# First two weight sets of a fused attention and two-layer gated MLP kernel, issued from ScalarE's DMA queue

## The chip, the cores and the metric

The kernel runs on one core of one Trainium2 chip. The metric is the device time of one execution in microseconds. Three timed runs of the kernel before gave 963.62 to 964.25 us, median 963.83 us.

## The reference, cut to what matters

Three stages, all in float32. Inputs `q`, `k`, `v` are (4, 8, 576, 64), and the five weight matrices are stored as 64-bit floats.

```python
# stage 1: attention, twice, then added
q_d, k_d, v_d = mean over groups of 4 positions            # 144 positions
out_d     = softmax(q_d @ k_d.T / 8) @ v_d                 # pooled attention
out_local = softmax(where(|i - j| < 4, q @ k.T / 8, -1e9)) @ v
x = repeat(out_d, 4) + out_local                           # -> (2304, 512)
# stage 2: gated layer, d_ff = 1536
g = x @ w_gate
y = (silu(g) * (x @ w_val)) @ w_out                        # (2304, 512)
# stage 3: leaky layer, d_ff = 2048
h = y @ w_in
out = (max(h, 0) + alpha * min(h, 0)) @ w2_out
```

## The kernel before, in words

Attention is cut into 32 units; unit `n` is half of the positions (288) of a pair of heads of one batch. Four units make one block of 288 tokens by 512 features, the input `xh`, `xl` of the gated layer (each float32 value is held as a high and a low float32r part, so that every product is three matmuls, `mm3`). The gated layer runs block by block, and within a block over 12 weight sets `j`. A set is three 512 KB loads: `g` (128 columns of `w_gate`), `v` (of `w_val`), `o` (128 rows of `w_out`). Before TensorE can use a loaded piece, `w_split` turns its 64-bit floats into the two parts: two passes on ScalarE (lines 129 and 137), one on VectorE (139), a copy on ScalarE (142) and a subtraction on GpSimd or VectorE (143). The split weights stay in SBUF for all eight blocks, so loading and splitting happen once, in the first 130 us or so; sets 0 to 3 have SBUF of their own, the later ones lie where data of the first eight units lay (`pslot`), and can be loaded only as these units finish.

The first eight units run before or beside block 0. Units 0 to 3 go through three loops in turn: transposes and scores (`a_T`, `a_QK`, `a_QE`), softmax (`a_EXP`, `a_NRM`), and the products with `v` (`a_vd`, `a_PT`, `a_PV`). Units 4 to 7 then run one after the other (`a_all`). Each unit needs its keys and queries (`a_load`), its pooled values (`a_load_v`), and windows of `v` (`a_load_w`, in the trace `qv<-vwin`), which are read from a DRAM buffer `vwin` that `stage` fills first by DRAM-to-DRAM copies. At the end `a_PV` writes `xh` and `xl`.

Order. All loads are issued by SyncE (`nc.sync`, in the trace `SPq`) on one queue, except two small copies at the start that ScalarE issues. The string `lo` in line 20 gives the order in which the first loads are written: `a` keys and queries of units 0 to 3, `s` and `t` the two halves of batch 0's `vwin`, `v` pooled values, `w` windows of units 0 to 3, `b` queries of units 4 to 7, `0` and `1` the weight sets 0 and 1, `x` windows of units 4 to 7, `2` and `3` the sets 2 and 3. The engines' instruction streams are in order; the stream of each engine is laid out by a list scheduler, which takes instructions by their place in the program as they become ready by its own estimates. `issue_after(i)` keeps what is inside it behind instruction `i` on the engine that issues `i`. `gate(n, stage)` notes the last VectorE, GpSimd and ScalarE instruction of unit `n` at the end of its scores (stage 0) or its softmax (stage 1); the splits of sets 0 and 1 stand behind the gates of unit 3, stage 1, on all three engines (`gD`, `gP`, `gA` are 8 for them). Sets 4 to 9, the load of `alpha`, batch 1's `vwin` and the loads of unit 8 (`load8`) follow on the same queue; sets 10 and 11, and the `vwin` copies of batches 2 and 3, are written after the tenth set has been split.

PSUM is shared: the banks of unit 3 (`gv`) become the banks of the first `g` and `v` products of the gated layer, so block 0 cannot begin before unit 3's product has been read.

Of the kernel before, what the change touches and what calls it, by code (L numbers as in the profile page):

```python
# [16 lines left out]
DRAM = bass.MemoryType.DRAM  # L17


K = dict(kdP=0, qdP=0, dnP=2, ldn=9, lo='asvtwb01x23', NPRO=8, c=5, a1=1, a2=0, OFF=25, oT=3, oE=3, oP=5, oV=12, vd1=2, vd2=1, pre=(0, 2, 0, 0), lo1=0, lo2=1, nst=3, nrm=0, sub=0, nrm1=0, sub1=0, qtA=0, ldw=1, xl1=0, ly=4, l2=3, st2=2, early=1, w2p=1, la=0, bdV=0, sp=9, s2=0, s3=0, gj=7, gs=1, vr=0, kc=0, gD=(8, 8, 0, 0, 0, 0), gP=(8, 8, 8, 8, 0, 0), gA=(8, 8, 0, 0, 0, 0))  # L20


@with_exitstack
def attn_moe_moe2_kernel(
# [13 lines left out]
    nc = tc.nc  # L38
# [24 lines left out]
    wp = ctx.enter_context(tc.tile_pool(name="wp", bufs=1))  # L63
# [33 lines left out]
    wdma = {}  # L97
    W = {}

    def w_load(kind, j, slot, pool=wp):  # L100
        t = raw[slot] = pool.tile([128, 512, 2], I32, tag=slot, name="raw", bufs=1)
        src = wsrc[kind]
        if kind in ("o", "o2"):
            r = nc.sync.dma_start(out=t.rearrange("p f t -> p (f t)"), in_=src[j * 128:(j + 1) * 128, :])
        else:
            r = nc.sync.dma_start(
                out=t.rearrange("p f t -> p (f t)").rearrange("p (k f) -> p k f", k=KD),
                in_=src[:, j * 256:(j + 1) * 256].rearrange("(k p) f -> p k f", p=128))
        wdma[slot] = r.ins
# [44 lines left out]
    def coords(n):  # L154
        blk, hp = divmod(n, NP)
        b, half = divmod(blk, 2)
        return b, half, hp, blk

    order = [f"{kind}{j}" for j in range(F1 - 8, F1) for kind in "gvo"]
    st_slots = order[5 * NP:][:K["nst"]]  # L160
    NEARLY = F1 - 2
    pslot = {(what, n): order[4 * i + n] for i, what in enumerate(("qv", "qs", "kn", "vd", "bd")) for n in range(NP)}
    for n in range(NP):
        pslot["qv", n + NP] = pslot["kn", n]
        pslot["qs", n + NP] = pslot["qs" if K["vr"] else "vd", n]
    NPRO = K["NPRO"]
    srs = [ap_.tile([128, 8], F32, name=f"sr{i}", bufs=1) for i in range(4)]
# [120 lines left out]
    def a_T(n, A):  # L288
# [24 lines left out]
        else:  # L313
            for r in range(NW):
                nc.tensor.transpose(A[:, 0, QB * r:QB * (r + 1)], d["qn"][:, r].rearrange("p h c -> p (h c)"), idn)
            if K["qtA"]:
                nc.scalar.copy(out=qT[:, 0:HB], in_=A[:, 0, 0:HB])
# [18 lines left out]
    def a_vd(n):  # L336
        b, half, hp, blk = coords(n)
        if n < NPRO and K["vr"]:
            return
        if half == 0:  # L340
            vs = vss[hp] = ap_.tile([72, 2, 2, D], F32, tag=f"vs{hp}", name="vs", bufs=1)
            for f in range(2):
                if n < NP:
                    nc.vector.reduce_sum(vs[:, f], hu[n]["vd"][f].rearrange("p h (r c) -> p h c r", r=4), axis=AX.X)
                    continue
                vv = hu[n]["vd"][f].rearrange("p h (r c) -> p h r c", r=4)
                nc.gpsimd.tensor_tensor(out=vv[:, :, 0:2], in0=vv[:, :, 0:2], in1=vv[:, :, 2:4], op=ALU.add)
                nc.gpsimd.tensor_tensor(out=vs[:, f], in0=vv[:, :, 0], in1=vv[:, :, 1], op=ALU.add)
# [10 lines left out]
    def a_QK(n, A):  # L359
        b, half, hp, blk = coords(n)  # L360
        d = hu[n]
        qT, kT, qd, kd = d["qT"], kTs[hp], d["qd"], kds[hp]
        with behind(n):
            for w in range(NW):
                for h in range(2):
                    hs = slice(64 * h, 64 * h + 64)
                    for i in range(NS):
                        q0 = QB * w + SUB * i
                        k0 = half * HB + q0
                        nc.tensor.matmul(A[SWIN * i:SWIN * (i + 1), h, w * SWIN:(w + 1) * SWIN],  # L370
                                         qT[hs, q0:q0 + SWIN], kT[hs, k0:k0 + SWIN], start=True, stop=True)
            for h in range(2):
                hs = slice(64 * h, 64 * h + 64)
                nc.tensor.matmul(A[:72, h, LW:SW], qd[hs], kd[hs], start=True, stop=True)

    def a_QE(n, A):
        half, d = coords(n)[1], hu[n]
        sm = late(n, "sm", [128, 2, SW])
        mx = d["mx"] = ap_.tile([128, 8], F32, tag="mx", name="mx", bufs=4)
        d["A"] = A  # L380
        mk = mask[:, half:half + 3].rearrange("p w j -> p (w j)").unsqueeze(1).to_broadcast([128, 2, LW])
        nc.vector.tensor_tensor(out=sm[:, :, 0:LW], in0=A[:, :, 0:LW], in1=mk, op=ALU.add)
        nc.vector.reduce_max(mx[:72, 6:8], A[:72, :, LW:SW], axis=AX.X)
        loc = d["loc"] = sm[:, :, 0:LW].rearrange("p h (w j) -> p h w j", w=NW)
        m4 = mx[:, 0:6].rearrange("p (h w) -> p h w", h=2)
        nc.vector.tensor_reduce(out=m4, in_=loc, axis=AX.X, op=ALU.max)
        d["act"] = K["a1" if n < 2 * NP else "a2"]
        d["la"] = n < NPRO and K["la"]
        if d["la"]:
            lb = d["lb"] = ap_.tile([128, 8], F32, tag="lb", name="lb", bufs=4)  # L390
            nc.vector.tensor_scalar(out=lb[:, 0:6], in0=mx[:, 0:6], scalar1=-scale, scalar2=None, op0=ALU.mult)
        if d["act"]:
            nb = d["nb"] = ap_.tile([72, 4], F32, tag="nb", name="nb", bufs=4)
            nc.vector.tensor_scalar(out=nb, in0=mx[:72, 4:8], scalar1=-scale / 16.0, scalar2=None, op0=ALU.mult)
        else:
            nc.vector.tensor_tensor(out=sm[:72, :, LW:SW], in0=A[:72, :, LW:SW],
                                    in1=mx[:72, 6:8].unsqueeze(2).to_broadcast([72, 2, SD]), op=ALU.subtract)
        if not d["la"]:
            (nc.vector if K["sub1" if n < NPRO else "sub"] else nc.gpsimd).tensor_tensor(out=loc, in0=loc, in1=m4.unsqueeze(3).to_broadcast([128, 2, NW, SWIN]), op=ALU.subtract)

    def a_EXP(n):
        d = hu[n]
        sm, A = d["sm"], d["A"]
        sr = d["sr"] = srs[n % 4]
        if d["act"]:
            for h in range(2):
                nc.scalar.activation(out=sm[:72, h, LW:SW], in_=A[:72, h, LW:SW], func=AF.Exp, scale=scale / 16.0,
                                     bias=d["nb"][:, 2 + h:3 + h], accum_out=sr[:72, 6 + h:7 + h])
        if d["la"]:
            for h in range(2):  # L410
                for w in range(NW):
                    c = NW * h + w
                    nc.scalar.activation(out=d["loc"][:, h, w], in_=d["loc"][:, h, w], func=AF.Exp, scale=scale,
                                         bias=d["lb"][:, c:c + 1], accum_out=sr[:, c:c + 1])
        else:
            nc.scalar.activation(out=sm[:, :, 0:LW], in_=sm[:, :, 0:LW], func=AF.Exp, scale=scale)
        if not d["act"]:
            nc.scalar.activation(out=sm[:72, :, LW:SW], in_=sm[:72, :, LW:SW], func=AF.Exp, scale=scale / 16.0)
# [92 lines left out]
            if kk == 1 and live:  # L511
                tick(6, HB)

    def load1(j):
        for kind in "gvo":
            w_load(kind, j, f"{kind}{j}")

    gates = {}

    def gate(n, stage):  # L520

        bb = tc.nc.cur_bb.bb.instructions
        for key, eng in (("D", nc.vector), ("P", nc.gpsimd), ("A", nc.scalar)):
            gates[key, n, stage] = next(i for i in reversed(bb) if i.engine == eng.engine)
# [613 lines left out]
    gs = {}  # L1138
# [171 lines left out]
    if True:  # L1310
# [65 lines left out]
        for n in range(NP):  # L1376
            a_T(n, P[n])
            a_QK(n, P[n])
            a_QE(n, P[n])
            gate(n, 0)  # L1380
        for n in range(NP):
            a_EXP(n)
            a_NRM(n)
            gate(n, 1)
        for n in range(NP):
            with tc.issue_after(gates["D", NP - 1, 0]):
                a_vd(n)
            a_PT(n, P[n])
            a_PV(n, P[n])
# [18 lines left out]
        for j in range(4, F1 - 2):  # L1408
            load1(j)
# [30 lines left out]
        OFF = K["OFF"]  # L1440
        at(0 if NPRO == NP else OFF - 7, lambda: a_pre(NPRO))
        for n in range(NPRO, NHU):
            if n < 2 * NP:
                c = K["c"]
                p, oT, oE, oP, oV = c * (n - NP) + 1, 1, 1, c - 1, c
            else:
                p, oT, oE, oP, oV = OFF + K["sp"] * (n - 2 * NP), K["oT"], K["oE"], K["oP"], K["oV"]
# [150 lines left out]
```

## Time and profile before

| what | value |
|---|---|
| median of 3 runs | 963.83 us |
| profiled execution | 963.16 us, its span 961.4 us |
| TensorE matmul busy | 923.8 us (96%) |
| VectorE, ScalarE, GpSimd busy | 627.4, 430.6, 370.9 us |
| granted TensorE clock, mean | 0.988 |
| DMA | 116.25 MB, mean 121 GB/s |

The profiled execution is 0.67 us under the median. TensorE works nearly all the time over the whole span; in the first eighth it does not, and the other engines and the DMA are at their busiest there. Views by stretch and the chain of waits tell more than the shares of the whole span, because the change touches loads of the first part alone.

### The profile page before, as it was taken

The numbers are of one execution on the slowest core, as the hardware profiler recorded it, in microseconds if no ns is written. First come the engines' busy times: TensorE is split into PE (matmuls) and PEld (weight loads), VectorE is DVE, ScalarE is ACT, GpSimd is POOL, SyncE is SP. The second block draws the span as 40 slices with busy tenths as digits, with TensorE's granted clock in tenths as the row PEclk, the third lists the DMA queues.
The fourth block names the chain that finished last, engine by engine and source line by source line (L and its number), as shares of the span: only waits on it lengthen the run. The fifth ranks groups of instructions, "written<-read, shape, count | busy, mean of one in ns | idle before, by whom it ended". The sixth has DMA issues, their size and how long they took to land.

```text
span 961.4 us, 20968 instructions
## 1 busy us (share of the span) xinstructions
PE 923.8 (96%) x8258; PEld 869.4 (90%) x8258; DVE 627.4 (65%) x1215; ACT 430.6 (45%) x965; POOL 370.9 (39%) x492
## 2 busy tenths in 40 slices
PE   6689889999999999999999998999999999999998
PEld 4478789999999999999999998999999988888887
DVE  5887775556454555545443365777767899688885
ACT  4698732222232222322222356664345775545553
POOL 7488863233422244322222278856161930000000
PEclk9689999999999999999999999999999999999999
DMA  7999741123111141111101346234426873445331
GB/s 193 267 339 364 178 104 28 37 66 63 43 46 24 35 92 36 35 41 22 49 10 39 111 137 210 109 119 156 161 111 213 294 280 97 154 142 164 113 110 44
DMA packets 162089, 116.25 MB, mean 121 GB/s; under 512 B 98889, under 2 KB 143177, under 8 KB 161225
## 3 DMA queue, kind: packets, MB, share of 16 engines
q1 hardware_dynamic: 161927, 114.92, 39.7%
q8 instruction: 64, 1.05, 0.5%
q14 instruction: 34, 0.28, 0.1%
q10 hardware_dynamic: 64, 0.01, 0.0%
HBM read 86.58 MB, written 34.60 MB: 126 GB/s over the span
## 4 chain that ended last, share of the span: by engine, by line
PE 82%; DMA 5%; SPq 4%; POOL 3%; DVE 2%; ACT 2%; issue 2%; DVEq 0%; POOLq 0%; ACTq 0%
PE y L1214 5%; PE y L503 5%; PE y L505 4%; PE g L505 4%; PE v L503 4%; PE y L504 4%; PE g L503 4%; PE g L504 4%; PE v L505 4%; PE c L1214 4%; PE v L504 4%; PE y L1013 3%; PE y L1014 3%; PE y L1015 3%; PE c L1013 3%; PE c L1014 3%
## 5 line engine op out<-in xcount | busy, mean ns | idle before, releaser
L547 DVE SCALAR_TENSOR_TENSOR u<-u,g 128x288 f32<-128x288 f32 x90 | 40.7, 452 | 134.0 <-ACT u L546 133.9
L503 PE MATMUL g<-xh,w 128*128 128x288 f32 x360 | 108.7, 302 | 10.9 <-DVE u L547 5.5
L505 PE MATMUL g<-xh,w 128*128 128x288 f32 x360 | 107.9, 300 | 1.2 <-POOL w L143 1.2
L504 PE MATMUL g<-xl,w 128*128 128x288 f32 x360 | 107.8, 299 | 0.0
L503 PE MATMUL v<-xh,w 128*128 128x288 f32 x360 | 107.6, 299 | 0.1
L504 PE MATMUL v<-xl,w 128*128 128x288 f32 x360 | 106.9, 297 | 0.0
L505 PE MATMUL v<-xh,w 128*128 128x288 f32 x360 | 106.6, 296 | 0.0
L562 POOL TENSOR_TENSOR pl<-u,ph 128x288 fp32r<-128x288 f32 x84 | 70.1, 835 | 88.9 <-ACT ph L561 88.7
L503 PE MATMUL y<-ph,w 128*128 128x288 f32 x336 | 102.5, 309 | 0.0
L504 PE MATMUL y<-pl,w 128*128 128x288 f32 x336 | 99.3, 296 | 0.1
L505 PE MATMUL y<-ph,w 128*128 128x288 f32 x336 | 99.0, 295 | 0.0
L561 ACT CAST ph<-u 128x288 fp32r<-128x288 f32 x84 | 36.3, 432 | 117.3 <-DVE u L554 117.3
L503 PEld LDWEIGHTS g<-xh,w 128*128 128x128 f32 x360 | 68.7, 191 | 12.9 <-DVE u L547 6.4
L546 ACT ACTIVATE u<-g 128x288 f32<-128x288 f32 x90 | 36.8, 409 | 88.5 <-PE g L505 87.6
L1214 PE MATMUL y<-w,hs 128*128 128x512 f32 x216 | 75.8, 393 | 0.0
L1163 DVE TENSOR_TENSOR hs<-hr,hs 128x512 fp32r<-128x512 f32 x98 | 63.9, 687 | 17.5 <-ACT hs L1157 16.1
L505 PEld LDWEIGHTS g<-xh,w 128*128 128x128 f32 x360 | 69.1, 192 | 1.4 <-POOL w L143 1.4
L503 PEld LDWEIGHTS v<-xh,w 128*128 128x128 f32 x360 | 68.3, 190 | 0.8 <-DVE u L554 0.5
L504 PEld LDWEIGHTS g<-xl,w 128*128 128x128 f32 x360 | 69.0, 192 | 0.0
L505 PEld LDWEIGHTS v<-xh,w 128*128 128x128 f32 x360 | 68.4, 190 | 0.0
L504 PEld LDWEIGHTS v<-xl,w 128*128 128x128 f32 x360 | 68.2, 190 | 0.0
L554 DVE SCALAR_TENSOR_TENSOR u<-u,v 128x288 f32<-128x288 f32 x90 | 40.8, 453 | 40.2 <-PE v L505 39.3
(296 smaller groups left out, 2814.7 us busy)
## 6 DMA issues: line engine op xcount, KB each, us to landing
hbuf<-t SPq DMA_DIRECT2D x64, 288.0 KB
hr<-hbuf SPq DMA_DIRECT2D x36, 512.0 KB
raw<-in_moe_w_out_dram SPq DMA_DIRECT2D x28, 512.0 KB
raw<-in_moe_w_in_dram SPq DMA_DIRECT2D x16, 512.0 KB
raw<-in_moe_w_gate_dram SPq DMA_DIRECT2D x12, 512.0 KB
raw<-in_moe_w_val_dram SPq DMA_DIRECT2D x12, 512.0 KB
vw<-vwin SPq DMA_DIRECT2D x48, 96.0 KB
sy<-y SPq DMA_DIRECT2D x8, 576.0 KB
```

The source lines that it names most:

```text
L503: nc.tensor.matmul(o, lhi, rhi, start=first, stop=False)
L504: nc.tensor.matmul(o, lhi, rlo, start=False, stop=False)
L505: nc.tensor.matmul(o, llo, rhi, start=False, stop=last)
L546: nc.scalar.activation(out=u, in_=G[:, :HB], func=AF.Tanh, scale=0.5)
L547: nc.vector.scalar_tensor_tensor(out=u, in0=u, scalar=1.0, in1=G[:, :HB], op0=ALU.add, op1=ALU.mult)
L554: nc.vector.scalar_tensor_tensor(out=u, in0=u, scalar=0.5, in1=G[:, :HB], op0=ALU.mult, op1=ALU.mult)
L561: nc.scalar.copy(out=ph, in_=u)
L562: nc.gpsimd.tensor_sub(pl, u, f32(ph))
L1013: nc.tensor.matmul(o, whi[:, ks], yhi[k], start=first, stop=False, skip_group_check=True)
L1014: nc.tensor.matmul(o, whi[:, ks], ylo[k], start=False, stop=False, skip_group_check=True)
L1163: vec[0].tensor_sub(t[:, 1], R[b][SRC[m]], f32(t[:, 0]))
L1214: nc.tensor.matmul(o.rearrange("p (e c) -> p e c", e=2), t[:, 0, i], w, start=first, stop=False, skip_group_check=True)
```

## The change

Sets 0 and 1 leave SyncE's list: `lo` has no `0` and `1` any more, so the order there is now queries of units 4 to 7, windows of units 4 to 7, sets 2 and 3. `w_load` and `load1` take the queue to issue from. `on_act`, called after each `gate` of units 0 to 3, issues set 0's three loads from ScalarE (`nc.scalar`) behind the last ScalarE instruction of unit 0's softmax, and set 1's three loads behind that of unit 2's softmax. The gates of the splits are as before.

```diff
-K = dict(kdP=0, qdP=0, dnP=2, ldn=9, lo='asvtwb01x23', NPRO=8, ...
+K = dict(kdP=0, qdP=0, dnP=2, ldn=9, lo='asvtwbx23', NPRO=8, ...
...
-    def w_load(kind, j, slot, pool=wp):
+    def w_load(kind, j, slot, pool=wp, queue=nc.sync):
...
-            r = nc.sync.dma_start(out=t.rearrange("p f t -> p (f t)"), in_=src[j * 128:(j + 1) * 128, :])
+            r = queue.dma_start(out=t.rearrange("p f t -> p (f t)"), in_=src[j * 128:(j + 1) * 128, :])
...
-            r = nc.sync.dma_start(
+            r = queue.dma_start(
...
-    def load1(j):
-        for kind in "gvo":
-            w_load(kind, j, f"{kind}{j}")
+    def load1(j, queue=nc.sync, kinds="gvo"):
+        for kind in kinds:
+            w_load(kind, j, f"{kind}{j}", queue=queue)
+
+    def on_act(n, stage):
+        for x in ACTQ.get((n, stage), ()):
+            with tc.issue_after(gates["A", n, stage]):
+                load1(int(x[0]), nc.scalar, x[1:])
+
+    ACTQ = {(0, 1): ["0gvo"], (2, 1): ["1gvo"]}
...
             gate(n, 0)
+            on_act(n, 0)
         for n in range(NP):
             a_EXP(n)
             a_NRM(n)
             gate(n, 1)
+            on_act(n, 1)
```

## Rows read from the trace of the kernel before

**Rows 1.** By stretch: us; busy us (instructions) per engine; granted clock; DMA share; GB/s.

```profile
12.00:30.00 18.00, 11.61 (x218) 8.08 (x216) 15.56 (x39) 8.46 (x32) 7.78 (x19) 1.00 0.71 209
34.00:90.00 56.00, 47.16 (x549) 42.51 (x550) 46.64 (x96) 52.12 (x124) 46.10 (x50) 0.82 1.03 340
60.00:93.00 33.00, 32.42 (x325) 30.92 (x324) 26.20 (x44) 29.83 (x68) 29.34 (x28) 0.99 1.05 377
93.00:127.00 34.00, 25.48 (x210) 22.65 (x210) 28.71 (x52) 21.61 (x43) 27.29 (x27) 0.97 0.71 175
...
130.00:300.00 170.00, 170.00 (x1901) 162.78 (x1900) 89.39 (x233) 47.11 (x119) 59.94 (x107) 1.00 0.22 51
```

**Rows 2.** Chain that ended last, in time: start us, us, what.

```profile
30.53 0.47 SPq L106
...
33.17 9.60 DMA raw<-in_moe_w_out_dram
...
57.98 8.52 DMA vwin<-in_v_dram
66.56 9.62 DMA raw<-in_moe_w_gate_dram
...
87.91 6.77 SPq L206
...
100.22 4.37 DMA raw<-in_moe_w_val_dram
...
110.57 1.31 POOL w L143
...
111.90 5.48 DMA raw<-in_moe_w_out_dram
...
123.81 1.23 POOL w L143
```

**Rows 3.** Timeline of ScalarE: start, us, instruction, [idle before <-releaser].

```profile
12.86 0.72 ACT L440 ACTIVATE qs<-qs,sr 72x144 f32<-72x144 f32 x2
15.48 0.32 ACT L310 COPY qs<-gv 128x192 f32<-128x192 f32 x1 [1.90 <-PE gv L309]
...
28.41 0.23 ACT L484 ACTIVATE qs<-att 128x72 f32<-128x72 f32 x1 [3.22 <-PE att L480]
...
34.55 0.66 ACT L129 ACTIVATE st<-raw 128x512 f32<-128x512 f32 x1 [0.39 <-DMA raw<-in_moe_w_gate_dram]
...
36.00 0.66 ACT L129 ACTIVATE st<-raw 128x512 f32<-128x512 f32 x1 [0.25 <-DMA raw<-in_moe_w_val_dram]
...
47.20 0.68 ACT L129 ACTIVATE st<-raw 128x512 f32<-128x512 f32 x1 [0.30 <-DMA raw<-in_moe_w_gate_dram]
```

**Rows 4.** ScalarE's two DMA issues, by line: count, ns min/median/max, first and last start.

```profile
L273 ACTq DMA_DIRECT2D vwin<-in_v_dram x1: 587/587/587, 0.7 to 0.7; - x1
L274 ACTq DMA_DIRECT2D vwin<-in_v_dram x1: 528/528/528, 1.4 to 1.4; - x1
```

**Rows 5.** Timeline of SyncE's queue: the window loads.

```profile
18.76 8.65 SPq L249 DMA_DIRECT2D qv<-vwin  x7
...
33.76 9.39 SPq L249 DMA_DIRECT2D qv<-vwin  x8
```

**Rows 6.** Timeline of VectorE around the end of the first units.

```profile
24.23 7.79 DVE L344 TENSOR_REDUCE vs<-vd 72x128 f32<-72x512 f32 x8
31.94 0.34 DVE L425 TENSOR_REDUCE sr<-qs 128x6 f32<-128x192 f32 x1
32.20 0.44 DVE L485 TENSOR_TENSOR qs<-att,qs 128x288 f32<-128x288 f32 x1
```

**Rows 7.** Timeline of TensorE: two of its waits late in block 0.

```profile
123.40 0.40 PE L503 MATMUL g<-xh,w 128*128 128x288 f32 x1 [1.21 <-ACT w L142]
125.09 0.45 PE L505 MATMUL g<-xh,w 128*128 128x288 f32 x1 [1.16 <-POOL w L143]
```

**Rows 8.** SyncE's waits, 46 to 86 us: us in total, times, longest.

```profile
SPq L106 <- DMA vwin<-in_v_dram: 4.7, 2, 2.8
```

More of the change, by code (lines that the diff above doesn't have):

```diff
@@ L17 @@
 DRAM = bass.MemoryType.DRAM
-K = dict(kdP=0, qdP=0, dnP=2, ldn=9, lo='asvtwb01x23', NPRO=8, c=5, a1=1, a2=0, OFF=25, oT=3, oE=3, oP=5, oV=12, vd1=2, vd2=1, pre=(0, 2, 0, 0), lo1=0, lo2=1, nst=3, nrm=0, sub=0, nrm1=0, sub1=0, qtA=0, ldw=1, xl1=0, ly=4, l2=3, st2=2, early=1, w2p=1, la=0, bdV=0, sp=9, s2=0, s3=0, gj=7, gs=1, vr=0, kc=0, gD=(8, 8, 0, 0, 0, 0), gP=(8, 8, 8, 8, 0, 0), gA=(8, 8, 0, 0, 0, 0))
+K = dict(kdP=0, qdP=0, dnP=2, ldn=9, lo='asvtwbx23', NPRO=8, c=5, a1=1, a2=0, OFF=25, oT=3, oE=3, oP=5, oV=12, vd1=2, vd2=1, pre=(0, 2, 0, 0), lo1=0, lo2=1, nst=3, nrm=0, sub=0, nrm1=0, sub1=0, qtA=0, ldw=1, xl1=0, ly=4, l2=3, st2=2, early=1, w2p=1, la=0, bdV=0, sp=9, s2=0, s3=0, gj=7, gs=1, vr=0, kc=0, gD=(8, 8, 0, 0, 0, 0), gP=(8, 8, 8, 8, 0, 0), gA=(8, 8, 0, 0, 0, 0))
 @with_exitstack
```

## The prediction

> **What bounds the kernel now.** I read the busy time by stretch first. From 130 to 300 us TensorE is busy for 170.00 of 170 us [rows 1]: whatever happens there costs TensorE time, and the change touches nothing of it. So the change can be worth only what TensorE loses before 130 us. From 60 to 93 us it is full as well (32.42 of 33), and from 93 to 127 us it works for 25.48 of 34 us, that is, it loses 8.5 us [rows 1]. The second thing to see in the same rows is the DMA share: 0.71 from 12 to 30 us, 1.03 from 34 to 90 us (a share above 1 is the way the profile counts, and means full), 0.71 again after 93 us. The loads of sets 0 and 1 stand at the front of the full stretch, and there is room ahead of it. The third is ScalarE: 52.12 of 56 us busy from 34 to 90 us, so that in this stretch the splitting of the weights and the units' small work run into ScalarE as much as into the DMA.
>
> Then the chain that ended last. From 30.53 us it goes along SyncE issuing the six loads of sets 0 and 1, then from 33.17 on 9.60 us through the last of them until it lands at 42.77, then through SyncE's later issues, 8.52 us of a `vwin` copy, 9.62 us until a `g` load lands at 76.2, one single issue of unit 8's keys that takes 6.77 us at 87.91, 4.37 us to the landing of a `v` piece at 104.6, a split that ends at 111.88, 5.48 us for an `o` piece that could be issued only then, and the split of that to 125.04 [rows 2]. So the chain is SyncE's queue and the DMA for most of 30 to 100 us, although TensorE is full for 33 us of that: what the queue delays shows only behind 93 us. The last two TensorE waits on the chain's end are 1.21 and 1.16 us [rows 7].
>
> The profiled execution took 963.16 us, its span 961.4; I sum against it and add the 0.67 us by which it lies under the median of 963.83.
>
> **The change part by part.**
>
> *Six issues on ScalarE.* The only issues of ScalarE in the trace took 0.587 and 0.528 us [rows 4], and SyncE's issue of a `g` piece took 0.47 [rows 2], so three issues are 3 x 0.56 = 1.7 us. Set 0's stand behind unit 0's last softmax instruction, which ends at 13.58; ScalarE's next instruction starts at 15.48 after 1.90 us of idleness [rows 3]. The issues would end at 15.25: hidden with 0.2 us to spare. What is queued behind them is unit 3's copies of the transposed queries and keys, and units 1 and 2's exponentials, and for these VectorE waits with little slack, so every microsecond past 15.48 would go on to VectorE's 24.23 and from there to the end of the first units. Bounds: 0, and 1.5 us if each issue took double. I take 0, because three durations agree. Set 1's three issues follow unit 2's softmax. Behind them stand unit 3's exponentials, whose result VectorE takes up at 31.94 only, after 7.79 us of sums over the pooled values [rows 6]: cost 0, and even some microseconds would be covered.
>
> *3.15 MB more between 14 and 30 us.* Six times 512 KB is 3.15 MB; at the 377 GB/s of 60 to 93 us [rows 1] that is 8.3 us of a full DMA. Idle there are 0.29 of 18 us, 5.2 us. So what was loaded in this stretch can be pushed back by about 8.3 - 5.2 = 3.1 us, the windows of units 0 to 3 first of all, which SyncE issues from 18.76 to 27.41 [rows 5]. Unit 0's product ends at about 28.4, when ScalarE takes it up at 28.41 [rows 3]; it is wanted by VectorE at 32.20 only [rows 6], because VectorE is with the sums until 32.02. Cover: 32.20 - 28.64 = 3.6 us for unit 0. A 3.1 us delay fits in, with 0.5 us left. If that cover goes, VectorE stalls ahead of unit 3's normalization and block 0 starts later by the excess. Bounds: 0 to 2.5 us (a set's whole 4.2 us falling upon unit 0, and the second on the last window loads); I take 0.5 us, nearer to the row that shows the cover.
>
> The Trainium skill, "DMA: Bandwidth & Descriptors", section "Issuing engines are not separate DMA queues", says that DMAs of several issuing engines share the same 16 DMA engines and interleave, so that a second issuer saves only issue time. The trace agrees for 34 to 90 us, with a share of 1.03, and leaves room for another reading at 0.71 ahead of it [rows 1]. If the rule were all, the sum would hold 3 us of SyncE's issue time and no bandwidth.
>
> *Earlier landing of sets 0 and 1.* ScalarE waited 0.39 us for set 0's `g` and 0.25 us for its `v` [rows 3]. Both go: -0.64 us at the start of the splits. No more than that goes: the splits stay behind unit 3's softmax, and ScalarE comes from that at 34.16 (34.55 less 0.39). Late next is ScalarE itself.
>
> *What SyncE has left.* Its list is six issues shorter (from 30.53 to 33.76, 3.2 us), and the windows of units 4 to 7, whose eight issues took 9.39 us [rows 2, 5], have 3.15 MB less in front. At the pace of the seven at 18.76 (1.24 us each) the eight need 9.9 us at most, so sets 2 and 3 are issued some 3 us earlier. ScalarE waited 0.30 us for set 2's `g` at 47.20 [rows 3]: -0.30 us.
>
> *What that brings late.* From 34 to 93 us the DMA is full; with 8.3 us of its work taken out ahead, the pile in front of SyncE is smaller when the `vwin` copies of the later batches (8.52 us on the chain) and sets 5 to 9 come. The slots of these sets come free as the first units finish, so not all of 8.3 us passes on. The part that I take is the end of the chain: with the single 6.77 us issue [rows 2] some microseconds shorter, the `v` piece landing at 104.6 and the split that ends at 111.88 come earlier, and with them the last `o` piece. The two waits behind that, 1.21 + 1.16 = 2.37 us [rows 7], go. Bounds: 0 (VectorE, busy 28.71 of 34 us there, holds TensorE as before) and the whole loss of 8.5 us from 93 to 127 us.
>
> Sum: +0.5 - 0.64 - 0.30 - 2.37 = -2.8 us. 963.16 - 2.8 = 960.35 for such an execution, 961.0 us for the median.
>
> **The rivals.**
>
> *Hidden anyway.* For: in 34 to 90 us ScalarE is busy 93% of the time, so a load that lands earlier only waits longer to be split; TensorE is full from 60 to 93 us; after that VectorE is busy for 84% [rows 1]. Against: the chain runs along loads and issues where ScalarE's small waits do not show it [rows 2]. Then only the waits for data at 34.55, 36.00 and 47.20 count, less the 0.5 us: 963.83 - 0.94 + 0.5 = 963.4 us.
>
> *ScalarE stands at the DMA issue.* A DMA instruction waits in line with the arithmetic of the engine that issues it. SyncE shows such standing: 4.7 us in two waits for an earlier transfer, the longer 2.8 us [rows 8], and 8.65 us for seven window loads, 1.24 each [rows 5]. If set 0's issues on ScalarE meet one wait of 2.8 us, they end at 13.58 + 1.7 + 2.8 = 18.1 instead of 15.25, 2.6 us past the 15.48 at which ScalarE had to go on; VectorE gets the exponentials of units 1 and 2 later by that, and all of the first units shift. With the gains of 0.94 us kept and the late part lost, and the 0.5 us of the windows, that is +2.2 us, 966.0 us. It decides against the change from the point where the third issue ends later than 15.9 (15.48 plus 0.94 less 0.5) if the late part is lost, and than 18.3 if it is kept. Against it: the destinations are fresh, so nothing has to be freed for these six.
>
> *Packets take turns.* If the two queues share the engines by turns, the small pieces of the windows lose half of their pace while a weight set is under way. Two sets at 4.2 us each give up to 4.2 us on unit 0's and 1's windows, 0.6 us more than the cover: 963.83 + 0.6 - 0.94 = 963.5 us without the late part. The Trainium skill, "DMA: Bandwidth & Descriptors", section "Queues, rings and completion order", states turns by packet between queues; no row here shows two large queues at once.
>
> A thing without a sign: the streams are laid out again by a list scheduler, and a different order of ScalarE's and VectorE's instructions in 20 to 130 us may give or take a microsecond or two. It widens the range.
>
> **How the numbers follow.** Chances: the forecast 0.47; hidden anyway 0.21; packets take turns 0.10; standing at the issue, or an order as bad, 0.22. About 0.2%, 1.9 us, is what a measurement can tell from no change. The forecast's case is faster by more than that nearly always, its own range 957.5 to 962.2; hidden anyway and taking turns lie within 1.9 us; the last case is slower. So faster 0.47, same 0.31, slower 0.22. The range has to reach into the slower case: from 957.0 (most of the 8.5 us lost after 93 us gained) to 966.5.
>
> **What would show it.** Right: ScalarE's first three issues near 13.6 us and all six with no more than 0.7 us each; the copy after them at 15.5; the splits of set 0 starting without a wait; a DMA share nearer to 0.9 from 12 to 30 us; the first products with the gated layer's weights no later than before; unit 8's keys issued in less than 9 us and earlier than 86 us; and TensorE's loss between 93 and 127 us smaller by 2 us or more. Wrong: VectorE's eight sums beginning later than 24.2 or its next step stalling for the windows, the first such product later than before, or a loss after 93 us that is as large as before although the loads land earlier; in that last case ScalarE and VectorE held the end of block 0, not the queue.

## The result, and the profile after

The changed kernel takes 972.38 us, median of 4 runs (971.67 to 973.07); the kernel before, run beside it, 963.73 us (962.36 to 964.25). The ratio is 1.0088 with a 95% interval of 1.0075 to 1.0101: slower by 8.65 us, outside the range that the prediction gave. The profiled execution took 971.9 us, its span 970.1, that is 8.7 us more than before.

First, ScalarE's timeline of the changed kernel (start, us, instruction, and in brackets the idle time before it with what ended it). It answers to [rows 3].

```profile
12.74 0.72 ACT L440 ACTIVATE qs<-qs,sr 72x144 f32<-72x144 f32 x2
18.05 0.41 ACTq L106 DMA_DIRECT2D raw<-in_moe_w_gate_dram  x1
20.65 0.38 ACTq L106 DMA_DIRECT2D raw<-in_moe_w_val_dram  x1
23.02 0.35 ACTq L104 DMA_DIRECT2D raw<-in_moe_w_out_dram  x1
23.41 0.32 ACT L310 COPY qs<-gv 128x192 f32<-128x192 f32 x1 [9.95 <-DMA vd<-in_v_dram]
...
29.76 0.72 ACT L440 ACTIVATE qs<-qs,sr 72x144 f32<-72x144 f32 x2 [1.74 <-DVE sr L429]
36.01 0.46 ACTq L106 DMA_DIRECT2D raw<-in_moe_w_gate_dram  x1
37.02 0.46 ACTq L106 DMA_DIRECT2D raw<-in_moe_w_val_dram  x1
39.73 0.35 ACTq L104 DMA_DIRECT2D raw<-in_moe_w_out_dram  x1
40.18 0.38 ACT L407 ACTIVATE qs<-gv,nb 72x144 f32<-72x144 f32 x1 [9.70 <-DMA raw<-in_moe_w_gate_dram]
...
45.06 0.65 ACT L129 ACTIVATE st<-raw 128x512 f32<-128x512 f32 x1
```

The six issues are short, 0.35 to 0.46 us, and yet ScalarE does nothing else from 13.46 to 23.41 us and from 30.48 to 40.18. What the trace names as the end of these stretches is the landing of a transfer that the copy at L310 and the exponential at L407 don't read: a load of pooled values (`vd`) for the first, a `g` piece for the second. It is the DMA issues ahead of them that waited. The copy that started at 15.48 before starts at 23.41.

The instruction listing of the changed program (cut here; the number is the place in the engine's own list) says for what. Every DMA of SyncE and of ScalarE is given one of eight completion semaphores (counters that a DMA raises when it has landed, and on which instructions wait), in turn, in the order in which the scheduler laid out both engines' DMAs together; a DMA waits until the one eight places ahead in that common order, which used the same semaphore, has landed. Both engines draw on the same eight:

```
SyncE    15 L266 DMA vwin<-in_v_dram 7x12x2048 [waits DMAHW3]
SyncE    17 L227 DMA vd<-in_v_dram 72x4x256 [waits DMAHW5]
SyncE    19 L227 DMA vd<-in_v_dram 72x4x256 [waits DMAHW7]
ScalarE  19 L106 DMA raw<-in_moe_w_gate_dram [waits DMAHW3]      set 0, g
ScalarE  20 L106 DMA raw<-in_moe_w_val_dram  [waits DMAHW5]      set 0, v
ScalarE  21 L104 DMA raw<-in_moe_w_out_dram  [waits DMAHW7]      set 0, o
SyncE    28 L249 DMA qv<-vwin 128x3x64 [waits DMAHW3]
SyncE    33 L218 DMA qv<-in_q_dram 96x3x64 [waits DMAHW0, PE]
ScalarE  36 L106 DMA raw<-in_moe_w_gate_dram [waits DMAHW0]      set 1, g
```

So set 0's `g` waits for a copy into `vwin` that SyncE issued at 10.12 us, its `o` for the fourth `vd` load, whose issue ended at 14.47. That `vd` is what the trace names. Set 1's `g` waits for a query load of units 4 to 7, and the chain of the changed kernel shows that landing release it (start, us, what):

```profile
34.02 1.97 DMA qv<-in_q_dram
36.01 4.17 DMA raw<-in_moe_w_gate_dram
40.18 0.83 ACT qs L407 x4
```

34.02 + 1.97 = 35.99, and the `g` issue starts at 36.01. The step from the `g` piece to L407 is one of time only: L407 started when set 1's `o` had been issued, which by the listing waits for a window load. The other way round, SyncE's fifth of seven window loads (28 in the listing) has set 0's `g` eight places ahead, and SyncE's waits show it:

```profile
SPq L249 <- DMA raw<-in_moe_w_gate_dram: 0.4, 1, 0.4
```

Next VectorE and TensorE behind ScalarE: two timelines of the changed kernel, answering to [rows 6, 7].

```profile
25.71 0.35 DVE L425 TENSOR_REDUCE sr<-qs 128x6 f32<-128x192 f32 x1 [8.10 <-ACT qs L416]
...
32.05 7.72 DVE L344 TENSOR_REDUCE vs<-vd 72x128 f32<-72x512 f32 x8
41.29 0.35 DVE L425 TENSOR_REDUCE sr<-qs 128x6 f32<-128x192 f32 x1 [1.52 <-ACT qs L416]
42.00 0.46 DVE L485 TENSOR_TENSOR qs<-att,qs 128x288 f32<-128x288 f32 x1 [0.35 <-ACT qs L484]
```

```profile
55.92 0.61 PE L503 MATMUL g<-xh,w 128*128 128x288 f32 x1 [2.77 <-DVE qs L485]
...
133.30 0.40 PE L503 MATMUL g<-xh,w 128*128 128x288 f32 x1 [1.20 <-ACT w L142]
134.99 0.40 PE L505 MATMUL g<-xh,w 128*128 128x288 f32 x1 [1.15 <-POOL w L143]
```

and the first product of the gated layer in the kernel before:

```profile
45.50 0.61 PE L503 MATMUL g<-xh,w 128*128 128x288 f32 x1 [3.04 <-DVE qs L485]
```

Read the delay along the way, each number a start after less the start before. The copy L310: 7.93 us. VectorE's eight sums: 32.05 - 24.23 = 7.82. Behind the sums the second stretch of standing: the sums cover most of its 9.70 us, and VectorE waits 1.52 us for unit 3's exponentials; its reduction L425 is at 41.29 instead of 31.94, 9.35 late. The addition L485: 9.80. The first gated product: 55.92 - 45.50 = 10.42. Then almost nothing is made up for 80 us: the two TensorE waits of [rows 7] are there again, 1.20 and 1.15 us long, at 133.30 and 134.99, both 9.90 us later than before, 0.52 less than the first gated product. The whole block 0 was moved, with its waits in it.

The last product `y<-pp` of the gated layer (the line of the view by operation, count: ns min/median/max, first and last start; first the kernel before, then the changed one):

```profile
L503 PE MATMUL y<-pp,w x48: 293/295/397, 545.1 to 595.6; 128*128 128x288 f32 x48
```

```profile
L503 PE MATMUL y<-pp,w x48: 293/297/442, 554.5 to 605.4; 128*128 128x288 f32 x48
```

The last of these 48 starts 9.8 us later, and the span ends 8.7 us later; 0.6 us came back by the one and 1.1 us behind it. I did not follow these up; the four runs of either kernel lie 1.4 and 1.9 us apart.

Stretches of the changed kernel (us; busy us per engine PE, PEld, DVE, ACT, POOL; clock; DMA share; GB/s), answering to [rows 1]:

```profile
12.00:30.00 18.00, 6.66 (x169) 4.18 (x167) 7.40 (x27) 5.60 (x22) 6.67 (x16) 1.00 0.80 253
34.00:90.00 56.00, 43.82 (x520) 38.87 (x521) 46.83 (x99) 44.79 (x116) 38.79 (x48) 0.94 1.00 324
93.00:127.00 34.00, 29.52 (x243) 27.61 (x244) 26.60 (x42) 26.11 (x53) 29.38 (x26) 0.95 0.62 169
104.00:138.00 34.00, 27.04 (x218) 24.48 (x218) 29.09 (x53) 22.15 (x43) 28.12 (x28) 0.95 0.56 137
```

From 12 to 30 us TensorE works 6.66 us instead of 11.61, VectorE 7.40 instead of 15.56. The row for 93 to 127 us is a trap: 29.52 us busy instead of 25.48 looks like the predicted gain, but the poor end of block 0 now lies 10 us later, and the stretch moved along with it, 104 to 138 us, has 27.04: 2.5 of the 4.0 us were the shift, and 1.6 us remain, which I did not follow up. In the row for 34 to 90 us the granted clock is 0.82 before and 0.94 after (means over its two levels, 0.5 for 1.2 GHz and 1 for 2.4), so that 47.16 and 43.82 us of a busy TensorE don't measure the same work.

### The profile page after: what moved, and what is told of

It reads as the page before. It is cut to its first block, busy times and chain, and to the rows that moved or that the text cites. A ratio compares the mean times of both kernels' runs of the same rounds, so it can differ in the third digit from the quotient of the medians.

```text
span 970.1 us, 20973 instructions
## 1 busy us (share of the span) xinstructions
PE 925.9 (95%) x8258; PEld 872.1 (90%) x8258; DVE 626.4 (65%) x1215; ACT 429.7 (44%) x965; POOL 372.4 (38%) x492
## 4 chain that ended last, share of the span: by engine, by line
PE 84%; DMA 3%; POOL 3%; DVE 3%; issue 3%; SPq 2%; ACT 1%; DVEq 0%; POOLq 0%; ACTq 0%
PE y L1221 5%; PE y L503 5%; PE v L503 4%; PE v L505 4%; PE g L503 4%; PE v L504 4%; PE y L505 4%; PE g L505 4%; PE y L504 4%; PE g L504 4%; PE c L1221 4%; PE c L1020 3%; PE y L1020 3%; PE y L1021 3%; PE y L1022 3%; PE c L1021 3%
```

## The experiments

Theory A: ScalarE stands at its DMA issues, for transfers of SyncE that are eight places ahead; the weights' bytes don't matter. Theory B: the early bytes push back windows and queries that the first units want. Each kernel was timed against the kernel before, run on the same chip.

**Six small copies on ScalarE, no weights moved.**

```diff
 # kernel before, sets 0 and 1 stay in SyncE's list
+    def on_act(n, stage):
+        if (n, stage) in ((0, 1), (2, 1)):
+            with tc.issue_after(gates["A", n, stage]):
+                for i in range(3):
+                    nc.scalar.dma_start(out=tny[...], in_=alpha...[:16, i:i + 1])   # 64 bytes
```

> The kernel before, with six copies of 16 x 4 bytes issued from ScalarE at the two places of the change; all weight sets stay on SyncE. Theory A (ScalarE stands at each issue until the earlier transfer that used the same one of eight completion semaphores has landed): the bytes do not matter, ScalarE goes on after the first three at 19 to 21 us instead of 15.5, the first gated-layer product comes 4 to 8 us later than 45.5, time 968 to 972 us. Rival B (3.15 MB early push back the first units' values and windows): no bytes, no loss, 963 to 965 us.

971.31 us, ratio 1.0080 (1.0065 to 1.0096). ScalarE's timeline:

```profile
17.31 6.16 ACTq L523 DMA_DIRECT2D tny<-in_moe_alpha_dram  x3
23.52 0.32 ACT L311 COPY qs<-gv 128x192 f32<-128x192 f32 x1 [9.91 <-DMA vd<-in_v_dram]
...
33.75 1.49 ACTq L523 DMA_DIRECT2D tny<-in_moe_alpha_dram  x3
```

VectorE behind its sums, and the first gated product:

```profile
39.69 0.34 DVE L426 TENSOR_REDUCE sr<-qs 128x6 f32<-128x192 f32 x1
...
52.66 0.61 PE L504 MATMUL g<-xh,w 128*128 128x288 f32 x1 [2.56 <-DVE qs L486]
```

Six copies of 64 bytes bring 7.3 of the 8.65 us (the kernel before took 963.99 us beside it), with the first standing as long as with 1.5 MB (9.91 and 9.95 us) and the same `vd` load at its end. VectorE is 7.75 us late behind its sums and the first gated product 7.16. The second three issues end at 35.24, under the sums, and VectorE doesn't wait for them: the 1.52 us that set 1's place adds in the changed kernel is not there. Theory A holds; B can't explain this run.

**One small copy**, as above with one copy and behind unit 0's softmax only.

```diff
-        if (n, stage) in ((0, 1), (2, 1)):
+        if (n, stage) == (0, 1):
...
-                for i in range(3):
+                for i in range(1):
```

> The kernel before with a single copy of 64 bytes from ScalarE behind unit 0's softmax; it has to wait for the semaphore of the first large DRAM copy of the windows, which landed at 17.3 us in the run with six. A: ScalarE goes on at 17.5 instead of 15.5, about a quarter of the standing of three: 965 to 967 us. B: nothing lost, 963 to 965 us.

966.84 us, ratio 1.0035 (1.0022 to 1.0048).

```profile
17.48 0.32 ACT L311 COPY qs<-gv 128x192 f32<-128x192 f32 x1 [4.17 <-DMA vwin<-in_v_dram]
```

The first copy's place in the turn belongs to the `vwin` copy, and that is what the trace names now. ScalarE is 2 us late (17.48 against 15.48), the first gated product 1.72 (47.22), the time 3.5 us up; what the rest of the 3.5 us is, I did not follow up. One issue suffices to lose.

**Set 0 alone on ScalarE; set 1 alone on ScalarE.**

```diff
-K = dict(... lo='asvtwbx23', ...
+K = dict(... lo='asvtwb1x23', ...          # set 0 alone ('asvtwb0x23' for set 1 alone)
-    ACTQ = {(0, 1): ["0gvo"], (2, 1): ["1gvo"]}
+    ACTQ = {(0, 1): ["0gvo"]}              # {(2, 1): ["1gvo"]} for set 1 alone
```

> Only set 0 from ScalarE behind unit 0's softmax, set 1 from SyncE behind the queries of units 4 to 7. A: ScalarE stands from 13.5 to about 23 us as in the changed kernel, and that is most of the loss: 969.5 to 972 us. B: half of the bytes, half of the loss: about 968 us.

> Only set 1 from ScalarE behind unit 2's softmax, set 0 from SyncE. A: ScalarE stands for 7 to 9 us from 22.7 us, but VectorE is with the pooled sums until 32 us, so that nearly all of it is covered: 963.5 to 966 us. B: half of the bytes, half of the loss: about 968 us.

Set 0 alone: 969.26 us, 1.0060 (1.0042 to 1.0078), the standing 9.13 us, the first gated product at 52.11. The time lies just under the range that A was given and 1.3 us above B's number and does not part the two; the standing does. Set 1 alone: 973.44 us, 1.0103 (1.0084 to 1.0122), more than both together, where I expected that VectorE's sums would cover it. ScalarE with set 1 alone:

```profile
33.33 0.48 ACTq L106 DMA_DIRECT2D raw<-in_moe_w_gate_dram  x1
37.07 0.37 ACTq L106 DMA_DIRECT2D raw<-in_moe_w_val_dram  x1
41.50 0.35 ACTq L104 DMA_DIRECT2D raw<-in_moe_w_out_dram  x1
41.95 0.38 ACT L407 ACTIVATE qs<-gv,nb 72x144 f32<-72x144 f32 x1 [19.59 <-DMA qv<-vwin]
```

Eight places ahead of these three there are now loads that SyncE itself issues late, among them set 0's `v`, and a window of units 4 to 7. The standing is 19.59 us long, because ScalarE reaches its place early and SyncE's queue does not. The cover that the prediction gave to set 1 is real, nearly 8 us of sums, but the wait outlasts it.

**Three small copies behind unit 2's softmax only**, the same place without any weights.

```diff
-        if (n, stage) in ((0, 1), (2, 1)):
+        if (n, stage) == (2, 1):
```

> The kernel before, plus three 64-byte copies that ScalarE issues behind unit 2's softmax, the place of set 1's loads; all weight sets stay on SyncE. Theory A (a DMA issue stands until the DMA eight places ahead in the scheduled order has landed): the third copy follows a load of the weights on SyncE by eight places, so ScalarE stands from about 22.5 us to 36 or 38 us, past the 32 us to which VectorE's sums cover it; first gated product 5 to 7 us later than 45.50, time 968 to 972 us. Rival (the first place alone does the harm; standing at the second is covered by VectorE's sums, as the prediction said): 963 to 965 us.

974.96 us, 1.0123 (1.0101 to 1.0145).

```profile
32.99 7.28 ACTq L523 DMA_DIRECT2D tny<-in_moe_alpha_dram  x3
40.38 0.38 ACT L408 ACTIVATE qs<-gv,nb 72x144 f32<-72x144 f32 x1 [17.88 <-DMA raw<-in_moe_w_gate_dram]
```

192 bytes in all, and the third largest loss of the study. The transfer named is set 1's `g` load on SyncE, the one that counting eight places gives. Standing was longer than I had put it (40.38, not 36 to 38), and the time lies above the 968 to 972 us expected; the first gated product comes at 56.15, 10.65 us late, and the time is 10.74 us up.

**Set 0 from ScalarE at unit 3's exponentials**, meant for a stretch where ScalarE idles.

```diff
+    ACTQ = {(3, 0.5): ["0gvo"]}            # set 1 on SyncE, lo='asvtwb1x23'
...
             a_EXP(n)
+            gate(n, 0.5)
+            on_act(n, 0.5)
             a_NRM(n)
```

> Only set 0 from ScalarE, but behind unit 3's exponentials at about 25 us, where ScalarE of the kernel before is idle until 28.4 us and its next results are wanted at 32 us. A: it stands again, until 29 to 32 us, but covered: 963 to 966 us. B: same bytes as with set 0 behind unit 0, only later: 966 to 969 us.

978.74 us, 1.0159 (1.0142 to 1.0176): my expectation failed again.

```profile
23.35 0.36 ACT L416 ACTIVATE qs<-qs 128x192 f32<-128x192 f32 x1
38.36 0.41 ACTq L106 DMA_DIRECT2D raw<-in_moe_w_gate_dram  x1
38.81 0.38 ACT L407 ACTIVATE qs<-gv,nb 72x144 f32<-72x144 f32 x1 [15.10 <-DMA raw<-in_moe_w_out_dram]
```

The issue did not land where it was meant to. The gate holds it behind unit 3's last exponential in the program's order, L416, and the scheduler had put L416 ahead of L407: the first issue stands between the two, ahead of unit 3's pooled exponentials, where ScalarE of the kernel before is idle for only 0.49 us (its L407 starts at 24.35). So the run does not show what an issue in an idle stretch costs. It shows again that the wait is for whatever stands eight places ahead, here set 1's `o` load. The first gated product is 6.2 us late (51.71), less than half of the 15.4 us lost; from 60 to 150 us TensorE works 75.48 us instead of 80.90, and I did not follow this up.

**Set 0 from ScalarE at the very start**, behind unit 0's scores, when few transfers are under way.

```diff
+    ACTQ = {(0, 0): ["0gvo"]}              # set 1 on SyncE, lo='asvtwb1x23'
```

> Only set 0 from ScalarE, behind unit 0's scores instead of its softmax, at about 7 us. A: the transfers that it waits for are small and have landed, so ScalarE stands less than 1.5 us in a stretch where it is idle for 2.9 us; but SyncE now has to wait for these three 512 KB loads at its own semaphores, so the windows' DRAM copies are issued 3 to 5 us later: 965 to 969 us. Without a coupling of the two queues SyncE's issues stay where they are: 963 to 965 us.

971.64 us, 1.0089 (1.0074 to 1.0104), above the 965 to 969 us expected. The three issues start at 5.95, 6.45 and 7.00 us with no standing, and now it is SyncE that waits, for ScalarE's weights (SyncE's waits up to 40 us: total, times, longest):

```profile
SPq L218 <- DMA raw<-in_moe_w_gate_dram: 2.2, 1, 2.2
SPq L260 <- DMA raw<-in_moe_w_val_dram: 1.4, 1, 1.4
...
SPq L227 <- DMA raw<-in_moe_w_out_dram: 0.2, 1, 0.2
```

The first `vwin` copy leaves at 13.38 instead of 9.13 us, and TensorE waits 5.61 us for unit 0's windows. Two queues that share the semaphores hold each other in both directions. But SyncE's own order had changed too: five query loads of units 4 to 7 now stand ahead of the first window load, which left at 15.23 us before.

```profile
19.47 8.23 SPq L218 DMA_DIRECT2D qv<-in_q_dram  x5
27.74 0.47 SPq L249 DMA_DIRECT2D qv<-vwin  x1
```

How much of this loss is the coupling (3.8 us of waits in the rows above), how much the bytes in front of the units' data, and how much the order, this run does not part.

**Both sets issued by GpSimd**, whose DMAs by the listing wait for none of the eight.

```diff
-            with tc.issue_after(gates["A", n, stage]):
-                load1(int(x[0]), nc.scalar, x[1:])
+            with tc.issue_after(gates["P", n, stage]):
+                load1(int(x[0]), nc.gpsimd, x[1:])
```

> Both sets at the same places, issued from GpSimd behind its own last instruction of the same softmax; GpSimd's transfers have semaphores of their own, so that nothing stands for another landing. A: the same bytes early and no loss from standing: 962 to 966 us. B: the bytes cost as in the changed kernel: 970 us or more.

983.42 us, 1.0196 (1.0179 to 1.0213). ScalarE does not stand, and the first gated product comes at 48.41; but TensorE waits 3.93 us for windows, and from 60 to 150 us it is busy for 70.08 us (80.90 before, 80.95 in the changed kernel). The order of VectorE's instructions had become another one. By the number the run falls to B (970 us or more), not to A (962 to 966). It shows that with the issue by GpSimd ScalarE does not stand, and does not settle what costs so much.

**Both sets early, on SyncE** (theory B by itself: no issue on ScalarE).

```diff
-K = dict(... lo='asvtwb01x23', ...
+K = dict(... lo='asvt0w1bx23', ...
...
-                with tc.issue_after(wlast[0]):
+                with tc.issue_after(wlast[0]) if wlast[0] else ExitStack():   # set 0 now comes ahead of the windows
                     load1(int(tok))
```

> Both sets as early as in the change but issued from SyncE: set 0 ahead of the windows of units 0 to 3, set 1 ahead of the queries of units 4 to 7; ScalarE issues nothing new. A (standing of ScalarE is the loss): ScalarE goes on at 15.5 us, the windows land up to 4.2 us later, which 3.6 us of cover takes in: 962.5 to 966 us. B (the early bytes cost by themselves): 969 us or more.

970.94 us, 1.0082 (1.0058 to 1.0106). ScalarE's copy L310 starts at 15.63, without standing. TensorE's waits, and VectorE behind its sums:

```profile
31.50 1.44 PE L480 MATMUL att<-bd,qv 128*64 128x96 f32 x11 [4.55 <-DMA qv<-vwin]
33.40 0.46 DVE L485 TENSOR_TENSOR qs<-att,qs 128x288 f32<-128x288 f32 x1 [1.06 <-ACT qs L484]
40.38 0.71 PE L315 MATMUL att<-ident,qv 96*128 96x96 f32 x3 [3.63 <-DMA qv<-in_q_dram]
...
49.11 0.61 PE L503 MATMUL g<-xh,w 128*128 128x288 f32 x1 [1.76 <-DVE qs L485]
```

So early weight bytes cost too, by another way, as B had it: windows and the queries of units 4 to 7 come late, and the first gated product is 3.6 us later. Of the windows' lateness most is covered: ScalarE takes up unit 0's product at 33.14 instead of 28.41, 4.73 us late, and VectorE's addition L485 starts 1.20 us late. The time is 7.6 us up, more than the first gated product is late; from 60 to 150 us TensorE works 77.90 us instead of 80.90, which I did not follow up.

**Both sets between the windows and the queries**, on SyncE.

```diff
-K = dict(... lo='asvtwb01x23', ...
+K = dict(... lo='asvtw01bx23', ...
```

> SyncE alone issues, the sets 0 and 1 stand behind the windows of units 0 to 3 but ahead of the queries of units 4 to 7. Theory B (early weight bytes cost because what they push back is wanted too): the queries land about 3 us later, units 4 to 7 begin later, part of it is covered since the windows of units 0 to 3 are not touched: 964 to 967 us, between before and early_on_sp (970.94). If only the windows matter: 963 to 964 us.

968.77 us, 1.0056 (1.0037 to 1.0074), a little above what B was given. TensorE at 41.57 us:

```profile
41.57 0.71 PE L315 MATMUL y<-ident,qv 96*128 96x96 f32 x3 [7.22 <-DMA qv<-in_q_dram]
```

The queries of units 4 to 7 alone account for the lateness of the first gated product (49.03).

**Set 2 ahead of the windows of units 4 to 7**, on SyncE, an attempt at a gain.

```diff
-K = dict(... lo='asvtwb01x23', ...
+K = dict(... lo='asvtwb012x3', ...
```

> SyncE alone issues, set 2 moves ahead of the windows of units 4 to 7, nothing else. The prediction's small terms (ScalarE waits 0.30 us for set 2's first piece) would give 963 us, 0.3 to 1 us less than before. Theory B: the windows of units 4 to 7 come some 4 us later; units 4 to 7 run one after the other beside block 0, so the delay either has cover (962.5 to 964) or costs up to 4 us (964 to 968).

964.22 us, 1.0002 (0.9990 to 1.0013), 12 runs: the same. No version here beats the kernel before.

**Sets 0 and 1 with an eighth of their bytes.**

```diff
+        if kind in ("g", "v", "o") and j < 2:
+            wdma[slot] = nc.sync.dma_start(out=t[:, :64]..., in_=src[r0:r0 + 128, c0:c0 + 128]).ins
+            return
...
+        rpt = lambda v: v[:, :64].unsqueeze(1).to_broadcast([128, 8, 64])   # what the splits read
```

> The kernel before, with each of the six loads of the sets 0 and 1 cut to an eighth of its bytes (64 KB instead of 512 KB); the splits read these columns eight times over, so the gated layer's result is left wrong. Queue places and engines as before. The bound on all that the change could give by taking 3.15 MB out of the full stretch: by the prediction's terms (0.64 + 0.30 + 2.37 us) 960 to 961 us, by the rival that the landing is hidden anyway 963 to 964 us.

970.66 us, 1.0071 (1.0053 to 1.0090): neither theory's number. Up to the first gated product the missing bytes are worth at most 0.72 us (44.78 against 45.50); 0.14 of that was there at L310 already (15.34 against 15.48), before any weights were loaded. From 60 to 93 us TensorE then loses 4.2 us that it did not lose before:

```profile
60.00:93.00 33.00, 28.18 (x269) 26.36 (x268) 19.18 (x41) 25.21 (x60) 25.00 (x23) 0.84 0.93 334
```

against 32.42 us in [rows 1]; one TensorE wait is as long as that loss, and ahead of it ScalarE waits as long for a `g` load:

```profile
73.70 0.67 ACT L140 ACTIVATE st<-raw 128x512 f32<-128x512 f32 x1 [4.61 <-DMA raw<-in_moe_w_gate_dram]
...
79.03 0.85 PE L515 MATMUL y<-ph,w 128*128 128x288 f32 x2 [4.37 <-ACT ph L573]
```

ScalarE's longest wait for a load from 66 to 93 us was 0.37 us before. The scheduled order of ScalarE's and later of SyncE's instructions differs from before, and I can't say that the bytes have anything to do with it. As a bound on the late gain the run is inconclusive; up to the first gated product it gives one.

## Why the prediction was wrong, step by step

**The step that failed** is "Six issues on ScalarE", with the sentence "I take 0, because three durations agree" and the bound of 1.5 us. The durations are right: 0.35 to 0.46 us measured. What I left out of the step is the time ahead of them and between them: ScalarE stood for 9.95 and 9.70 us in all. The two issues in [rows 4], at 0.7 and 1.4 us, are among the first eight DMAs, which have none eight places ahead, and so could not show a wait for one. I had cited for SyncE 8.65 us for seven issues [rows 5] and 4.7 us of waits [rows 8], used them for a rival, and took neither as the bound.

**The rival "ScalarE stands at the DMA issue"** was the mechanism, with a chance of 0.22, and mis-sized: one wait of 2.8 us for set 0, when there are three in a row for each set. Its "against it: the destinations are fresh" looked at the wrong condition. Nothing had to be freed in SBUF; the completion semaphore had to be. Put with the measured size, the rival's 2.6 us past 15.48 become 7.93 at L310 for set 0, and 9.35 with what set 1 adds behind the sums. The single-place runs show that either place alone loses. The Trainium skill, "DMA: Bandwidth & Descriptors", section "Anatomy of one DMA — SWDGE (gpsimd) path", which is about DMAs that GpSimd issues, says that the DMA engines do not wait on semaphores, and that a wait is spent on the issuing sequencer before dispatch; the trace shows the same for ScalarE, 9.95 us with no arithmetic on it, and I had not drawn on it.

**"Set 1 ... cost 0, even some microseconds would be covered"**: the cover, nearly 8 us of sums, was there and limits set 1's part in the changed kernel to 1.52 us of VectorE's waiting; it was overrun at 17.88 and 19.59 us.

**The windows' 0.5 us, with a cover of 3.6 us**: not visible in the changed kernel, where ScalarE is later than the windows. By itself the step was about right: in `early_on_sp` TensorE waits 4.55 us for windows, unit 0's product is taken up 4.73 us late, and 1.20 us of that reach VectorE, as a cover of 3.6 us would have it. What the step lacked are the queries of units 4 to 7, which were not in my sum at all: TensorE waits 3.63 us for them there, and `weights_before_queries` shows that they can be the dearer (7.22 us).

**Set 0's and set 2's small waits (0.64 and 0.30 us)**: set 0's first split does start without a wait, but at 45.06. The run with an eighth of the bytes has 0.72 us less at the first product, not far from the 0.94 that I had, but one execution of each kernel is all that this compares.

**The tail, 2.37 us**: wrong. Part of what I named as its sign came true: the four issues of unit 8's keys take 4.74 us (9.15 before; one of the four was the 6.77 of [rows 2]). They start at 93.91, later than before in time, though 2.6 us earlier when counted from the first gated product (93.91 - 55.92 against 86.06 - 45.50). And yet both waits stayed, 1.20 and 1.15 us. A shorter queue at that place did not make the end of block 0 faster; the waits name the weights' copy on ScalarE and the subtraction on GpSimd, as they did before.

**"Hidden anyway"** is thereby what the bytes are worth as far as it could be measured: at most 0.72 us early; late the changed kernel shows no gain that I could trace to them, and the run with an eighth of the bytes is inconclusive. **"Packets take turns"** was not tested: no run isolates it.

What stays open: the 1.7 us that came back between the first gated product and the end; the split of `set0_on_act_first` into coupling, bytes and order; the losses behind 60 us in `sets_on_pool`, `set0_on_act_in_idle`, `early_on_sp` and `sets_0_1_an_eighth`. Every one of these kernels has an order of instructions of its own, laid out again by the scheduler, and no run holds that order fixed; the standing itself does not hang on it, since the listing and the traces name the transfer each time.

## What to carry to other kernels

A DMA issued by a computing engine is an instruction in that engine's line, and its price is the wait ahead of it, not its own length: ask for each which earlier transfer must have landed, and look at the longest of the busy queue's issues instead of the median of an idle one. If a framework deals out a small set of completion semaphores to all queues, a second queue is not independent of the first, so list them in order and count back. When a stage is moved in time, compare it by its own events, not by fixed windows: the stretch from 93 to 127 us showed a gain of 4 us, of which 2.5 were a shift. And when an instruction is meant for an idle stretch, look in the trace whether it got there: the gate names an instruction of the program's order, and the scheduler's order can be another.

## What the runs showed that I had not expected

- Three copies of 64 bytes and three loads of 512 KB cost ScalarE the same at the same place, 9.91 and 9.95 us of standing.
- The coupling works both ways: with three loads issued at 5.95 to 7.00 us by ScalarE, SyncE waited 2.2, 1.4 and 0.2 us for them.
- A later place can be dearer: 9.13 us of standing for set 0 behind unit 0's softmax, 15.10 between unit 3's exponentials, 19.59 for set 1 alone behind unit 2's softmax.
